# Three moves in a two-stage kernel: one x turned by crossbar, one attention started four steps later, one v loaded later

## The chip, the cores and the metric

The kernel runs on one core of a Trainium2 chip. The core has TensorE (PE, matmuls; its weight loads are shown apart as PEld), VectorE (DVE), ScalarE (ACT), GpSimd (POOL) and SyncE (SP). POOL and SP here mostly issue DMAs, which run on the core's 16 DMA engines. The metric is the device time of one execution in microseconds, lower being better; the figure used is the median of several executions.

## What is computed

Attention over four batches and eight heads, and then two matrix products with a leaky ReLU between them:

```python
# q, k, v: (4, 8, 768, 64); three "retrieval" heads (0, 2, 6) see all earlier keys,
# the other five see the first 4 keys ("sink") and the last 64 ("window")
scores = scale * np.matmul(q, k.transpose(0, 1, 3, 2))
...
scores = np.where(mask[None, :, :, :], scores, -1000000000.0)
scores = scores - np.max(scores, axis=-1, keepdims=True)
a = np.exp(scores)
a = a / (np.sum(a, axis=-1, keepdims=True) + 1e-09)
out = np.matmul(a, v)
...
x = out.transpose(0, 2, 1, 3).reshape(3072, 512)
h = x @ w_in                      # 512 -> 2048
g = np.maximum(0.01 * h, h)
return g @ w_out                  # 2048 -> 512
```

## The kernel before, in words

The 3,072 tokens are cut into eight chunks of 384, two for each batch, in the order of the list ORDER: chunks 0 and 1 are the first halves of batches 0 and 1, chunks 2 and 3 their second halves, then the same for batches 2 and 3. Every chunk goes through attention, product 1 (x times w_in, with the leaky ReLU on ScalarE) and product 2 (times w_out). The schedule is written out by hand: each stage is a list of small functions ("slots"), and helpers merge the lists, so that the order in the program is the order on each engine. Each engine works through its instructions in that order.

**Attention of a chunk** (class Attention, method slots). A unit is one group of scores. For a retrieval head in the second half of a batch there are five groups, in the first half two; a window head has one; and there is one sink group for all heads. That makes 21 units in a second half and 12 in a first half. A unit has two parts. qk makes the scores on TensorE into one bank of the tag psS, which has two banks (lines 329 and 364, sink line 309), has ScalarE take the exponential (lines 334, 369, 312), and has VectorE multiply by a mask where one is needed (lines 337, 339, 373). do_av, a few slots later (the lag), multiplies by v on TensorE (line 298, "sums" below). When the last unit of a pair of heads is through, finish divides by the sum on VectorE (lines 395 and 397) and leaves xs, with tokens on the partitions. Product 1 needs it turned, with features on the partitions; x_t does that, in one of two ways. On TensorE it makes three transposes against the identity into a bank (line 407), and ScalarE (line 409) or VectorE (line 411) copies the bank to xt. That takes place three slots after finish. With cross set, one DMA transpose issued from SP (line 402, the "crossbar") moves xs to xt at once, and the three extra slots are not there. Before the change chunks 1 to 3 turn x on TensorE (chunk 2 with ScalarE's copy, into the banks ph; chunk 3 with VectorE's, into the banks py), and chunks 4 to 7 by crossbar.

**Product 1** (in_slots) has 16 slots of four matmuls of 128x384 (line 563) into one of two banks ph; ScalarE applies the leaky ReLU (line 565). **Product 2** (out_slots) has 16 slots, called steps below, of two to four matmuls of 128x512 (line 589); 16 matmuls make a tile of 128 tokens. When a tile is whole, VectorE copies it to SBUF (line 595) and SP writes it out (line 596).

**Loads.** load_qk and load_v issue loads of k, q and v on POOL's queue (lines 113 and 118). turn_dma turns k and q with two DMA transposes on SP (line 228). spreads gives six copies on VectorE (line 237) that put the turned keys into the two key tiles kt, and for a first half two small ones of the sink keys (lines 262 and 266). v_shift makes, with two DMAs on SP (lines 145 and 146), the copy vb of v shifted by 64 tokens, which window heads read.

**The main loop** runs n from 2 to 7. Round n merges product 1 of chunk n and what is left of product 2 of chunk n - 1 with the attention of chunk n + 1. Its loads run ahead: it issues the turn, the shift and the spreads for chunk n + 2, and the loads of chunk n + 3. Ahead of the loop chunk 2's attention (a2) is merged with steps of product 2 of chunks 0 and 1 (o0 and o1). The merging deals the slots of attention evenly before the steps:

```python
want = (j + 1) * len(as_) // len(ms)
r += as_[done:want] + [m]
```

tail interleaves the last slots of two lists, and both joins a slot with one of the copies of spreads, which is how chunk 4's key copies stand inside chunk 3's attention before the change. into puts such copies between the slots of later attentions.

Of the kernel before, what the change touches and what calls it, by code (L numbers as in the profile page):

```python
# [21 lines left out]
def kernel(  # L22
# [12 lines left out]
    nc = tc.nc  # L35
# [23 lines left out]
    def bank(tag, shape, dtype):  # L59
        return ps.tile(shape, dtype, name=tag, tag=tag, bufs=BANKS[tag])  # L60

    def bf(name, *shape):
        return one.tile([128, *shape], BF16, name=name)
# [14 lines left out]
    m_win = bf("m_win", 6, 64)  # L78
    m_win0 = bf("m_win0", 6, 64)
    m_sink = bf("m_sink", H)  # L80
    shift = bf("shift", 2, 128)
    kt = [[bf(f"kt{i}_{hh}", 4, S) for hh in range(2)] for i in range(2)]
    va = [bf(f"va{i}", 6, H, D + 1) for i in range(B)]
# [23 lines left out]
    def load_qk(n, nms="kq"):  # L107
        b, c = ORDER[n]
        for nm in nms:
            t = rot.tile([128, 3, H, D], BF16, name=f"{nm}b", tag=f"{nm}b", bufs=1)  # L110
            raw[nm, n] = t
            for g in range(3):
                nc.gpsimd.dma_start(out=t[:, g], in_=nat[nm][b, c, :, :, g])  # L113

    def load_v(n, gs=range(3)):
        b, c = ORDER[n]
        for g in gs:
            nc.gpsimd.dma_start(out=va[b][:, 3 * c + g, :, 0:D], in_=nat["v"][b, c, :, :, g])  # L118
# [3 lines left out]
    def load_sinks(b, eng=None):  # L122
        vsf[b] = rot.tile([32, D], FP32, name="vsf", tag="vsf", bufs=2)
        (eng or nc.sync).dma_start(out=vsf[b][:], in_=v[b, :, 0:NS, :])

    def sink_values(b, eng):
        n = H - 1
        eng.tensor_tensor(
            vs[b % 2][0:32, 1:H, 0:D],
            vsf[b].rearrange("p (o d) -> p o d", o=1).to_broadcast([32, n, D]),  # L130
            m_sink[0:32, 1:H].rearrange("p (h o) -> p h o", o=1).to_broadcast([32, n, D]),
            op=ALU.mult)
# [8 lines left out]
    def v_shift(n, eng=None):  # L141
        eng = eng or nc.sync
        i, c = ORDER[n]
        lo, hi = (0, 2) if c == 0 else (2, 5)
        eng.dma_start(out=vb[i][0:64, lo:hi], in_=va[i][64:128, lo:hi])
        eng.dma_start(out=vb[i][64:128, lo:hi], in_=va[i][0:64, lo + 1 : hi + 1])
# [77 lines left out]
    def turn_dma(n):  # L224
        qx[n] = rot.tile([128, 3, 4, 128], BF16, name="qd", tag="qd", bufs=3)
        raw["kx", n] = rot.tile([128, 3, 4, 128], BF16, name="kd", tag="kd", bufs=2)
        for nm, dst in (("k", raw["kx", n]), ("q", qx[n])):
            nc.sync.dma_start_transpose(out=dst.rearrange("p g q t -> p (g q) t"),
                                        in_=raw[nm, n].rearrange("p g h d -> p (g h d)"))

    def spreads(n):
        b, c = ORDER[n]

        def spread(g, hh):
            r = slice(64 * hh, 64 * hh + 64)
            o = CH * c + 128 * g
            nc.vector.tensor_copy(kt[b % 2][hh][r, :, o : o + 128], raw["kx", n][r, g])  # L237

        r = [lambda g=g, hh=hh: spread(g, hh) for g in range(3) for hh in range(2)]
        if c == 0:  # L240
            r += sink_keys_by(b)
        return r
# [4 lines left out]
    def into(slots, extra):  # L247
        r, extra = [], list(extra)
        for j, s in enumerate(slots):
            r.append(s)  # L250
            if 5 * j >= 2 * len(slots) and extra:
                r.append(extra.pop(0))
                if len(extra) > len(slots) - j - 2:
                    r.append(extra.pop(0))
        return r + extra
# [19 lines left out]
    xts = {}  # L275
# [279 lines left out]
    py = {}  # L555

    def in_slots(n, tags=("ph",)):
        def tick(t):
            if n not in gs:
                gs[n] = rot.tile([128, NG, CH], BF16, name="g", tag="g", bufs=2)  # L560
            ph = bank(tags[t % len(tags)], [128, 512], FP32)
            for g in range(KG):
                nc.tensor.matmul(ph[:, 0:CH], lhsT=w_in_bf[:, g, 128 * t : 128 * t + 128],  # L563
                                 rhs=xts[n][:, g, :] if n else xts[0][:, :, g, :], start=(g == 0), stop=(g == KG - 1))
            nc.scalar.activation(out=gs[n][:, t, :], in_=ph[:, 0:CH], func=ACTF.Prelu, alpha=0.01)  # L565

        return [lambda t=t: tick(t) for t in range(NG)]
# [14 lines left out]
    def out_slots(n, tags=("py", "py", "py"), halves=False):  # L582
        slots = []

        def part(tt, lo, hi, tag, c0, c1):
            if lo == 0:
                py[n] = bank(tag, [128, 512], FP32)
            for ng in range(lo, hi):
                nc.tensor.matmul(py[n][:, 0 : c1 - c0], lhsT=gs[n][:, ng, 128 * tt : 128 * tt + 128],  # L589
                                 rhs=w_out_bf[:, ng, c0:c1], start=(ng == 0), stop=(ng == NG - 1))  # L590
            if hi == NG:
                o = rot.tile([128, DM], FP32, name="o", tag="o", bufs=6)
                b, c = ORDER[n]
                r0 = S * b + CH * c + 128 * tt
                nc.vector.tensor_copy(o[:, 0 : c1 - c0], py[n][:, 0 : c1 - c0])  # L595
                nc.sync.dma_start(out=out[r0 : r0 + 128, c0:c1], in_=o[:, 0 : c1 - c0])

        for tt in range(3):
            if halves and tt == 2:
                slots.append(lambda: part(2, 0, NG, "py", 0, 256))  # L600
                slots.append(lambda: part(2, 0, NG, "psS", 256, 384))
                slots.append(lambda: part(2, 0, NG, "po", 384, 512))
                continue
            lo = 0
            for w in ([3, 3, 3, 3, 4], [3, 3, 3, 3, 4], [3, 3, 3, 3, 2, 2])[tt]:
                slots.append(lambda tt=tt, lo=lo, w=w: part(tt, lo, lo + w, tags[tt], 0, DM))
                lo += w
        return slots

    def run(*lists):  # L610
        for l in lists:
            for f in l:
                f()

    def tail(ms, a):

        return [a[0], ms[0], a[1], ms[1], a[2], ms[2], ms[3], *a[3:]]

    def both(s, e):
        return lambda: (s(), e and e())  # L620

    def merge(ms, as_):

        r, done = [], 0
        for j, m in enumerate(ms):
            want = (j + 1) * len(as_) // len(ms)
            r += as_[done:want] + [m]
            done = want
        return r + as_[done:]
# [152 lines left out]
    o0, o1 = out_slots(0), out_slots(1)  # L782
# [1 line left out]
    run(spreads(2))  # L784
    run(o0[6:12])
    v_shift(3)
    a2, m2 = Attention(2, xt_tag="ph").slots(lag=3), o0[12:] + o1[0:10]
    run(merge(m2[:10], a2[:-6]), tail(m2[10:], a2[-6:]))
    run(spreads(3))
    outs = o1[10:]  # L790

    for n in range(2, NCH):
        a, extra = [], ()
        if n + 2 < NCH:
            turn_dma(n + 2)
            v_shift(n + 2)
            extra = spreads(n + 2)
            if ORDER[n + 2][1] == 0:
                load_sinks(ORDER[n + 2][0], nc.gpsimd)
                sink_values(ORDER[n + 2][0], nc.gpsimd)  # L800
            if n + 3 < NCH:
                load_qk(n + 3)
                load_v(n + 3)
        if n + 1 < NCH:
            a = Attention(n + 1, xt_eng="v", xt_tag="py", cross=n > 2).slots(lag=2 if n > 2 else 3)
            a = into(a, extra) if n > 2 else a
        ms = merge(in_slots(n), outs)
        keep = []
        if n == 2:
            a = [both(s, e) for s, e in zip(a, [None] * 16 + extra + [None] * 3)]  # L810
            ms, a, keep = ms[:-6], a[:-6], tail(ms[-6:-2], a[-6:]) + ms[-2:]
        elif a:
            ms, keep = ms[:-9], ms[-9:]
            if n > 4:
                keep.insert(1, a.pop())
        run(merge(ms, a), keep)
        outs = out_slots(n) if n + 1 < NCH else out_slots(n, ("psS", "psS", "py"), True)
    run(outs)

# [34 lines left out]
```

## Time and profile before

| What | us |
|---|---|
| median of 5 runs (lowest 233.71, highest 235.93) | 234.3 |
| the profiled execution, whole | 235.93 |
| its span, from first to last instruction | 234.1 |
| TensorE busy | 226.7 |
| ScalarE busy | 127.7 |
| VectorE busy | 98.0 |
| POOL busy | 71.3 |

The profile shows one execution. Times of single rows are microseconds from the start of the span; a row of a timeline gives start, duration, engine, line, operation and how many equal instructions it merges, and in brackets how long the engine was idle before it and what released it. Matmuls are pipelined: the duration of a row has a fixed latency in it, and the time that a matmul takes from its engine is the distance to the start of the next. These are the stretches that the change touches:

| Stretch, us | What runs on TensorE |
|---|---|
| 48 to 56 | product 2 of chunk 0 alone |
| 56 to 73 | chunk 2's attention with product 2 of chunks 0 and 1 |
| 73 to 95 | round 2: chunk 3's attention, product 1 of chunk 2, rest of product 2 of chunk 1 |
| 95 to 120 | round 3: chunk 4's attention, product 1 of chunk 3, product 2 of chunk 2 |
| 120 to 145 | round 4: chunk 5's attention, product 1 of chunk 4, product 2 of chunk 3 |

### The profile page before, as it was taken

Reading aid. Unit: us, or ns where it says so; the run is one execution under the profiler, and the core shown is the slowest. Engines: PE = TensorE matmul, PEld = TensorE weight load, DVE = VectorE, ACT = ScalarE, POOL = GpSimd, SP = SyncE. Lnnn points to the kernel's source line nnn. Section 1 sums busy time; section 2 is a strip of 40 time slices with the busy share of each in tenths; the row PEclk is TensorE's granted clock in tenths of the full one; section 3 lists DMA queues with packets and bytes.
Section 4 is the critical chain, followed back from the end, with each engine's and each line's share of the span. In section 5 each row is a group of like instructions: output and inputs, shape, how many; then the busy total and the mean of one; then the engine's idle time right before and its main releaser. Section 6 shows DMA issues by size and latency. Waiting matters only on the chain.

```text
span 234.1 us, 5117 instructions
## 1 busy us (share of the span) xinstructions
PE 226.7 (97%) x2080; PEld 140.9 (60%) x2080; DVE 98.0 (42%) x282; ACT 127.7 (55%) x275; POOL 71.3 (30%) x87
## 2 busy tenths in 40 slices
PE   7888999999999999999999999999999999999995
PEld 5668776644665676566556665666656665555554
DVE  7793668115465358446313551156211351111122
ACT  5765875722774786655355545765556763434300
POOL 8967544118419239359004900000000000000000
PEclk9997999999999999999999999999999999999999
DMA  9999999999999999999959991920220221111112
GB/s 129 148 166 178 203 207 168 177 122 154 141 213 230 178 174 122 183 165 164 127 120 184 173 164 44 221 72 17 64 62 0 64 74 25 45 45 45 44 49 91
DMA packets 109480, 28.98 MB, mean 124 GB/s; under 512 B 101248, under 2 KB 105744, under 8 KB 109456
## 3 DMA queue, kind: packets, MB, share of 16 engines
q0 software_dynamic: 77088, 13.39, 75.7%
q1 hardware_dynamic: 31312, 15.00, 31.4%
q10 hardware_dynamic: 1056, 0.26, 0.5%
q8 instruction: 16, 0.26, 0.5%
q14 instruction: 8, 0.07, 0.1%
HBM read 27.30 MB, written 6.29 MB: 143 GB/s over the span
## 4 chain that ended last, share of the span: by engine, by line
PE 88%; POOL 4%; DMA 4%; DVE 2%; ACT 1%; issue 1%; POOLq 0%
PE py L589 32%; PE ph L563 29%; PE po L298 6%; PE psS L329 6%; DMA kb<-in_k_dram 4%; PE psS L589 3%; PE psS L364 3%; PE ph L576 2%; PE psS L563 2%; PE psS L309 2%; POOL va L118 1%; POOL k L104 1%; POOL q L105 1%; DVE xs L397 1%; POOL kb L113 1%; ACT at L334 1%
## 5 line engine op out<-in xcount | busy, mean ns | idle before, releaser
L589 PE MATMUL py<-w_out_bf,g 128*128 128x512 bf16 (+1 forms) x352 | 90.6, 374 | 0.0
L563 PE MATMUL ph<-xt,w_in_bf 128*128 128x384 bf16 x448 | 90.4, 326 | 0.0
L565 ACT ACTIVATE g<-ph 128x384 bf16<-128x384 f32 x112 | 55.0, 491 | 57.2 <-PE ph L563 56.9
L563 PEld LDWEIGHTS <-w_in_bf 128*128 128x128 bf16 x480 | 44.0, 98 | 30.7
L589 PEld LDWEIGHTS <-g 128*128 128x128 bf16 x416 | 35.8, 98 | 25.9
L334 ACT ACTIVATE at<-psS 128x384 bf16<-128x384 f32 x78 | 37.1, 488 | 17.4 <-PE psS L329 16.9
L595 DVE COPY o<-py 128x512 f32<-128x512 f32 (+1 forms) x22 | 14.9, 679 | 52.4 <-PE py L589 52.1
L113 POOL DMA_DIRECT2D kb<-in_k_dram x21 | 18.7, 906 | 37.2 <-DMA kd<-kb 36.5
L329 PE MATMUL psS<-qd,kt 128*128 128x384 bf16 (+2 forms) x90 | 23.3, 294 | 0.0
L118 POOL DMA_DIRECT2D va<-in_v_dram x24 | 21.4, 911 | 4.2 <-DVE xs L544 2.0
L113 POOL DMA_DIRECT2D qb<-in_q_dram x21 | 18.6, 908 | 5.6 <-DMA w_in_bf<-in_moe_w_in_dram 1.8
L298 PE MATMUL po<-va,at 128*128 128x65 bf16 x228 | 19.3, 194 | 0.0
L373 DVE TENSOR_TENSOR ats<-ats,m_win 128x384 bf16<-128x384 bf16 x35 | 13.2, 381 | 13.5 <-ACT ats L369 12.8
L369 ACT ACTIVATE ats<-psS 128x384 bf16<-128x384 f32 x35 | 16.9, 490 | 3.2 <-PE psS L364 2.9
L298 PEld LDWEIGHTS <-at 128*128 128x128 bf16 x234 | 14.9, 98 | 5.2 <-issue 0.2
L397 DVE TENSOR_TENSOR xs<-po,linv 128x384 bf16<-128x384 f32 x27 | 15.1, 557 | 0.9
L329 PEld LDWEIGHTS <-kt 128*128 128x128 bf16 x99 | 9.5, 98 | 7.7 <-issue 0.6
L364 PEld LDWEIGHTS <-kt 128*128 128x128 bf16 x210 | 10.5, 98 | 5.1 <-issue 0.2
L339 DVE TENSOR_TENSOR at<-at,m_caus 128x128 bf16<-128x128 bf16 x21 | 4.8, 240 | 20.6 <-ACT at L334 20.4
L237 DVE COPY kt<-kd 64x512 bf16<-64x512 bf16 x36 | 12.9, 359 | 0.6
L298 PEld LDWEIGHTS <-ats 128*128 128x128 bf16 x210 | 10.4, 97 | 4.1 <-DVE xs L397 0.4
L337 DVE TENSOR_TENSOR at<-at,m_caus 128x256 bf16<-128x256 bf16 x21 | 6.3, 298 | 14.7 <-ACT at L334 14.7
(145 smaller groups left out, 209.8 us busy)
## 6 DMA issues: line engine op xcount, KB each, us to landing
out_dram<-o SPq DMA_DIRECT2D x23, 256.0 KB, 2.4
va<-in_v_dram POOLq DMA_DIRECT2D x24, 128.0 KB, 7.4
kb<-in_k_dram POOLq DMA_DIRECT2D x21, 128.0 KB, 5.8
qb<-in_q_dram POOLq DMA_DIRECT2D x21, 128.0 KB, 5.8
w_in_bf<-in_moe_w_in_dram POOLq DMA_DIRECT2D x4, 512.0 KB, 9.8
w_out_bf<-in_moe_w_out_dram POOLq DMA_DIRECT2D x4, 512.0 KB, 13.6
vb<-va SPq DMA_DIRECT2D x8, 195.0 KB, 4.1
vb<-va SPq DMA_DIRECT2D x4, 130.0 KB, 3.5
```

The costliest lines, as they stand in the source:

```text
L113: nc.gpsimd.dma_start(out=t[:, g], in_=nat[nm][b, c, :, :, g])
L118: nc.gpsimd.dma_start(out=va[b][:, 3 * c + g, :, 0:D], in_=nat["v"][b, c, :, :, g])
L298: nc.tensor.matmul(o, lhsT=lhsT, rhs=rhs, start=first, stop=False, skip_group_check=True)
L329: nc.tensor.matmul(s[:, off : off + w], lhsT=kt[i][hh][:, p, 128 * kj : 128 * kj + 128], rhs=q_of(n, p, lo, CH), start=(j == 0), stop=(j = ...
L334: nc.scalar.activation(out=a[:, 0:off], in_=s[:, 0:off], func=ACTF.Exp, scale=SM)
L364: nc.tensor.matmul(s[:, 64 * m : 64 * m + 64], lhsT=kt[i][hh][:, p, k0 : k0 + 128], rhs=q_of(n, p, 64 * m, 64 * m + 64), start=(m == 0), s ...
L369: nc.scalar.activation(out=av_, in_=s[:, 0:CH].rearrange("p (j e f) -> p j e f", j=3, e=2), func=ACTF.Exp, scale=SM)
L397: nc.vector.tensor_tensor(xs[:], po[:, :, :, 0:D], linv.to_broadcast([128, 3, 2, D]), op=ALU.mult)
L563: nc.tensor.matmul(ph[:, 0:CH], lhsT=w_in_bf[:, g, 128 * t : 128 * t + 128], rhs=xts[n][:, g, :] if n else xts[0][:, :, g, :], start=(g == ...
L565: nc.scalar.activation(out=gs[n][:, t, :], in_=ph[:, 0:CH], func=ACTF.Prelu, alpha=0.01)
L589: nc.tensor.matmul(py[n][:, 0 : c1 - c0], lhsT=gs[n][:, ng, 128 * tt : 128 * tt + 128], rhs=w_out_bf[:, ng, c0:c1], start=(ng == 0), stop= ...
L595: nc.vector.tensor_copy(o[:, 0 : c1 - c0], py[n][:, 0 : c1 - c0])
```

## The change

Chunk 3's attention is built with cross set: its x is turned by four crossbar DMAs on SP instead of twelve transposes on TensorE and four copies on VectorE. Its list of slots has 24 entries instead of 27. Chunk 2's x is still turned on TensorE, but VectorE makes the copy instead of ScalarE. Ahead of the loop chunk 2's attention is merged with two steps fewer of chunk 1's product 2; they go to round 2. There the eight copies of chunk 4's keys no longer stand among the slots of chunk 3's attention but after all of the round's slots. Round 3 begins with four steps of chunk 2's product 2 alone, then merges four more, and product 1 of chunk 3 comes after these eight. Chunk 6's v is not loaded together with its q and k at the start of round 3; at the end of the round POOL copies one element of chunk 4's last part of xt to a new tile named hold, which makes the queue wait for that part to land, and then issues the load.

```diff
+    hold = bf("hold", 1)
...
-    def both(s, e):
-        return lambda: (s(), e and e())
...
-    a2, m2 = Attention(2, xt_tag="ph").slots(lag=3), o0[12:] + o1[0:10]
-    run(merge(m2[:10], a2[:-6]), tail(m2[10:], a2[-6:]))
+    a2, m2 = Attention(2, xt_tag="ph", xt_eng="v").slots(lag=3), o0[12:] + o1[0:8]
+    run(merge(m2[:8], a2[:-6]), tail(m2[8:], a2[-6:]))
     run(spreads(3))
-    outs = o1[10:]
+    outs = o1[8:]
...
                 load_qk(n + 3)
-                load_v(n + 3)
+                if n != 3:
+                    load_v(n + 3)
         if n + 1 < NCH:
-            a = Attention(n + 1, xt_eng="v", xt_tag="py", cross=n > 2).slots(lag=2 if n > 2 else 3)
+            a = Attention(n + 1, cross=True).slots(lag=2 if n > 2 else 3)
             a = into(a, extra) if n > 2 else a
-        ms = merge(in_slots(n), outs)
+        if n == 3:
+            run(outs[:4])
+            ms = outs[4:8] + merge(in_slots(n), outs[8:])
+        else:
+            ms = merge(in_slots(n), outs)
         keep = []
         if n == 2:
-            a = [both(s, e) for s, e in zip(a, [None] * 16 + extra + [None] * 3)]
-            ms, a, keep = ms[:-6], a[:-6], tail(ms[-6:-2], a[-6:]) + ms[-2:]
+            ms, a, keep = ms[:-6], a[:-3], tail(ms[-6:-2], a[-3:]) + ms[-2:]
...
-        run(merge(ms, a), keep)
+        run(merge(ms, a), keep, extra if n == 2 else ())
+        if n == 3:
+
+            nc.gpsimd.tensor_copy(hold[0:1, :], xts[n + 1][0:1, 3, 0:1])
+            load_v(n + 3)
```

## The prediction, written before the changed kernel was run

> **What bounds the kernel now.** I read the page's busy table first, then the granted clock, then TensorE's timeline from 48 us on for places where it stands still, and last the views of the engines that release it there.
>
> ```profile
> PE 226.7 (97%) x2080; PEld 140.9 (60%) x2080; DVE 98.0 (42%) x282; ACT 127.7 (55%) x275; POOL 71.3 (30%) x87
> ...
> PEclk9997999999999999999999999999999999999999
> ```
>
> TensorE (PE) is busy 97% of the span, at full clock but for one slice near 20 us, and the diff changes no instruction before 56 us. From there the end is TensorE's own work plus the moments when it stands still. Its row durations overlap, so I count from start to start: a 128x512 matmul takes 0.216 us (352 of them), 128x384 takes 0.162, 128x128 0.056, a sum of 65 columns 0.029. By these steps TensorE stands still for only 1.26 us between 48 us and the end: 0.15 (57.77), 0.06 (65.13), 0.23 (68.83), 0.09 (74.09), 0.06 and 0.13 (76.18 and 76.42), 0.47 (94.07) and 0.07 at 166. Two of these places matter. The first is in chunk 2's attention:
>
> ```profile
> 67.93 0.33 PE L329 MATMUL psS<-qd,kt 128*128 128x384 bf16 x1
> 68.09 0.25 PE L298 MATMUL po<-va,at 128*128 128x65 bf16 x3
> 68.18 0.33 PE L407 MATMUL ph<-ident,xs 128*128 128x128 bf16 x3
> 68.35 0.33 PE L329 MATMUL psS<-qd,kt 128*128 128x256 bf16 x2
> 68.51 0.26 PE L298 MATMUL po<-va,at 128*128 128x65 bf16 x3
> 68.83 0.34 PE L364 MATMUL psS<-qd,kt 128*128 128x64 bf16 x6
> ```
>
> ```profile
> 68.29 0.49 ACT L334 ACTIVATE at<-psS 128x384 bf16<-128x384 f32 x1 [0.85 <-PE psS L329]
> ```
>
> Scores rotate over two banks (psS). The score at 67.93 is read by ScalarE from 68.29 to 68.78, and the next but one, into the same bank, starts at 68.83 though TensorE had finished its steps by 68.51 + 3 x 0.029 = 68.60. So a score can follow the one two before it only 0.90 us later (0.36 to ScalarE, 0.49 there, 0.05 back). The second place is the end of chunk 3's attention:
>
> ```profile
> 92.30 1.46 PE L563 MATMUL ph<-xt,w_in_bf 128*128 128x384 bf16 x8
> 94.07 0.34 PE L407 MATMUL py<-ident,xs 128*128 128x128 bf16 x3 [0.31 <-DVE xs L397]
> 94.25 0.59 PE L589 MATMUL py<-w_out_bf,g 128*128 128x512 bf16 x2
> ```
>
> Eight matmuls from 92.30 are through at 93.60; the transposes start at 94.07, when VectorE has made xs.
>
> **Chunk 3's x by crossbar.** Twelve transposes (line 407) leave TensorE. Three take 0.17 us (88.60 to 88.77, 89.94 to 90.11): 12 x 0.056 = -0.67. The wait at 94.07 goes with them: -0.47. Four copies of 0.35 (line 411) leave VectorE, which bounds nothing. SP gains four transposes. They stand behind chunk 4's turn, its shift of v and an output, free from about 87; the first three pairs go there. The last pair's xs comes at about 93.4: sums finished at 92.4, reciprocal and product 0.20 + 0.56, nothing ahead of them on VectorE. After those sums TensorE has 9.2 us to do before chunk 3's product 1: three tiles of it for chunk 2 (1.95), 27 product-2 matmuls (5.83) and chunk 4's first scores and sums (1.45); the pair is read by the fourth matmul, 0.49 later. So it may take 8.6 us from issue. The view of line 402 has the price:
>
> ```profile
> L402 SPq DMA_TRANSPOSE xt<-xs x16: 1177/1180/2233, 102.9 to 196.2; - x16
> ...
> DMA to landing us min/median/max: 2.3/3.8/7.0
> ```
>
> All sixteen would be in time, so I take 0. The upper bound is the longest landing of the larger transposes (line 228), 11.1 us: 2.5 us late. Behind the pair on SP stand an output and chunk 5's turn; that output was issued at 95.60 before, and chunk 1's last tile is copied out at about 95.0 now, so these do not move later.
>
> The Trainium skill, page "VectorE: DVE Perf Modes", section "Rules for kernel authors", speaks against this part: transpose 128x128 on TensorE if a PSUM destination will do. The same page's section "The three transpose paths" has 390 ns there and 1309 ns by crossbar. The row says 56 ns of TensorE's time in a full queue. By the page's figure the part would be worth 12 x 0.39 = 4.7 us, an estimate; by the row 0.67.
>
> **Two product-2 steps out of chunk 2's attention.** m2 falls from 14 steps to 12, the merged ones from ten to eight, for the same 21 slots of attention. Before, a step (0.43 to 0.86 us of matmuls) stood after every two slots, and only the last group had three. Now five groups have three scores without a step between, and each third one meets the bank rule. The matmuls between first and third score are: slots 2 to 4, 0.56 with the second score's own wait of 0.15; slots 7 to 9, two scores and nine sums 0.59; slots 10 to 12, 0.50; slots 15 to 17, 0.76; slots 18 to 20, 0.67. The rest to 0.90 is lost: 0.34 + 0.31 + 0.40 + 0.14 + 0.23 = 1.42, and with the 0.15 that stays, 1.57. Before these were 0.15 + 0.06 + 0.23 = 0.44. This part costs +1.13. The bounds are 0 (the waits hide) and 1.13 plus 1.4, should the four copies of chunk 2's x, now VectorE's at 0.35 instead of ScalarE's at 0.49, stand ahead of masks that the sums wait for. VectorE is busy 7.0 of the 16 us from 56 to 72, and a mask is ready some 0.5 us before its sum, so I take 0 for the copies. The 0.06 at 65.13 came from such a copy on ScalarE and is in the sum.
>
> The removed steps run later: 0.65 us each wherever they stand, 0 in sum. In chunk 3's attention 18 tiles stand among 21 slots instead of 16, so no three scores meet. At its start 0.28 goes: x's last copy is 0.14 shorter, more than the 0.09 waited at 74.09, and chunk 3's six key copies (2.70 us from 73.99) no longer stand behind an output's copy of 0.69, which ends the 0.06 and 0.13.
>
> **Chunk 4's keys and its four steps.** The eight copies (six of 0.27 to 0.72, two of 0.54 and 0.16) move behind chunk 3's xs and an output's copy, to about 95.0. The first score that reads them comes after twelve matmuls (2.6 us), at about 97.4; it needs the first copy, done by 95.7. The third score group and the sink score have more. Cost 0. Without the four steps the score would come at 94.8 and wait 0.9. Those steps are the same matmuls, moved.
>
> **Chunk 6's v.** On POOL one element is copied when x(4) has landed (about 118), and three loads of 0.9 us follow, instead of at 108.55. Behind them on POOL are chunk 7's k and q, which waited for kd until 126.36 anyway. v lands after 4.3 to 14.2 us (line 118), so by 125 to 135. Behind it on SP stands the shift of v (125.11 before), then x(5), whose first pair went at 127.66 and whose last at 139.92. Chunk 5's product 1 starts at 145.93 and chunk 6's vb is read at 151.11. Even 135 leaves ten us. Cost 0. No gain either: x(4) landed 118.93 and was read from 120.95.
>
> **Sum.** -0.67 - 0.47 - 0.28 + 1.13 = -0.29 us. The span goes from 234.1 to 233.8. The profiled execution took 235.93 (1.83 around the span), so 235.6; it was the longest of the five runs. Against their median of 234.3 I subtract the same: 234.0.
>
> **Rivals.** First, the thinned attention costs nothing: -1.42, or 232.9. For it: ScalarE is busy only 10.25 of 16 us there, so on average it keeps up. Against it: 68.83 shows the wait in the one group of three that exists. Second, and on the other side, chunk 3's x lands late. The place is the fourth matmul of its product 1. The cost begins 8.6 us after issue, and it decides from 10.1 us on. At 11.1 us the time is 234.0 + 2.5 = 236.5. For it: loads of chunk 5's k, q and v and its turn share the DMA engines, busy over 90% in these slices, and larger transposes needed 11.1. Against it: sixteen of the same size had 7.0 at most, some under the same load. Third, the copies on VectorE delay sums: up to 1.4, or 235.4. Against it are the idle stretches of VectorE there. Fourth, the late load of v does nothing, as I count it; were it to speed up x(4), nothing waits for that.
>
> **How the numbers follow.** A measurement of this kernel tells 0.5% from no change, 1.17 us: below 233.1 is faster, above 235.5 slower. My forecast has 0.60 (own range 233.5 to 234.6), the first rival 0.22, the second 0.13, the third 0.05. Faster is the first rival, 0.22. Slower is the second and the third, 0.18: the third's full price ends within 0.1 us of the line, and I count it there. The rest is no change. The predicted time is 234.0. The range reaches down past the first rival, 232.7, and up to 235.3, near the third; the second stays out.
>
> **What would show it.** Right: no line 407 after 80 us and no wait near 94; five waits of 0.1 to 0.4 us between scores of line 329 and 364 from 57 to 69; product 1 of chunk 3 starting without a gap at about 101.6; v of chunk 6 landing after 122 with no gap after it. Wrong: scores in groups of three running without waits (then 232.9), or a gap before line 564 near 101 released by a DMA (then 235 and more).

## The result and the profile after

| | before | after |
|---|---|---|
| median, us | 234.03 (90 runs) | 234.58 (48 runs) |
| ratio, 95% interval | | 1.0036 [1.0023, 1.005] |
| the profiled execution, us | 235.93 | 234.35 |
| its span | 234.1 | 232.6 |
| first score of chunk 2's attention, from the start of the span | 56.48 | 55.02 |
| from there to the start of the last matmul ("middle") | 174.60 | 174.25 |
| from there to the end of the span ("tail") | 3.06 | 3.31 |

The change makes the kernel slower by 0.84 us (0.36% of 234.03; 0.54 to 1.17 by the interval). That is less than the 0.5% which the prediction called no change, but it is resolved, and its sign is not that of the forecast: 0.29 us less. The profiled execution of before happened to be a long one, with a granted clock of 0.97 instead of 1.00 before 56 us, so spans of single executions say little here. The medians are over all runs and lie only 0.55 us apart, while the ratio leaves disturbed executions out and counts that after has more long ones (17 of 48 above 235.3 us, against 8 of 90). The middle, which holds all that the diff moves, is 0.35 us shorter after, close to the 0.29 that was predicted from the same row of before; but these are two single executions, and over four traces of each the difference is 0.06 (see "What is left").

The first lines are of the page of after.

```profile
span 232.6 us, 5101 instructions
...
PE 224.5 (97%) x2068; PEld 138.9 (60%) x2068; DVE 96.4 (41%) x282; ACT 127.1 (55%) x271; POOL 71.8 (31%) x88
...
PEclk9999999999999999999999999999999999999999
```

TensorE has 12 instructions fewer, the transposes. It is still busy 97%, so the same way of counting holds: start to start, and what exceeds the steps of the prediction is standing still. The kernel after has one line more ahead of everything, so line 329 is now 330, and so on.

TensorE's timeline of after in chunk 2's attention (start, duration, engine, line, operation, and in brackets the idle time and its releaser):

```profile
61.07 0.33 PE L330 MATMUL psS<-qd,kt 128*128 128x256 bf16 x2
61.24 0.25 PE L299 MATMUL po<-va,at 128*128 128x65 bf16 x3
61.72 0.34 PE L365 MATMUL psS<-qd,kt 128*128 128x64 bf16 x6 [0.23 <-ACT at L335]
...
66.47 0.33 PE L330 MATMUL psS<-qd,kt 128*128 128x256 bf16 x2
66.63 0.26 PE L299 MATMUL po<-va,at 128*128 128x65 bf16 x3
66.95 0.34 PE L365 MATMUL psS<-qd,kt 128*128 128x64 bf16 x6
```

Three sums from 61.24 are through at 61.24 + 3 x 0.029 = 61.33; the score starts at 61.72, 0.40 later, released by the exponential. The pair at 66.63 and 66.95 loses 0.23 in the same way. All the waits of this stretch are 0.15 (56.30), 0.34 (56.89), 0.30 (59.84 and 60.14), 0.40, 0.13 (64.89) and 0.23: 1.55, where the prediction has 1.57 at the same five places and the one that stays.

Where product 1 of chunk 3 begins, in TensorE's timeline of after:

```profile
100.35 0.20 PE L299 MATMUL po<-va,ats 128*128 128x65 bf16 x1
100.39 0.81 PE L564 MATMUL ph<-xt,w_in_bf 128*128 128x384 bf16 x4
101.03 0.33 PE L330 MATMUL psS<-qd,kt 128*128 128x256 bf16 x2
```

The first matmul follows its neighbour by 0.04 and the four of them take 0.64: no wait for the x that the crossbar turns. SP's view has the four DMAs, and behind them the output and chunk 5's turn:

```profile
85.73 7.61 SPq L403 DMA_TRANSPOSE xt<-xs  x4
93.79 0.34 SPq L597 DMA_DIRECT2D out_dram<-o  x1
94.30 3.47 SPq L229 DMA_TRANSPOSE kd<-kb  x1
```

They landed at 92.3, 93.9, 96.2 and 99.1, the last 6.9 us after its issue at 92.2, where the prediction allowed 8.6.

One place that the prediction passed over is tight now. TensorE and POOL of after, where chunk 4's product 1 begins:

```profile
118.98 0.33 PE L330 MATMUL psS<-qd,kt 128*128 128x384 bf16 x1
119.14 0.81 PE L564 MATMUL ph<-xt,w_in_bf 128*128 128x384 bf16 x4
119.79 0.33 PE L330 MATMUL psS<-qd,kt 128*128 128x256 bf16 x2
```

```profile
119.25 0.18 POOL L821 COPY hold<-xt 1x1 bf16<-1x1 bf16 x1 [9.28 <-DMA xt<-xs]
119.49 2.64 POOL L119 DMA_DIRECT2D va<-in_v_dram  x3
```

POOL's copy of one element stands behind the landing of chunk 4's last part of x, and runs at 119.25. The fourth matmul of 119.14, which reads that part, starts 0.49 later, at 119.63. About 0.4 us are left. Before, x had landed at 118.93, 2.0 us ahead of the first of these matmuls.

### The profile page after: what moved, and what is told of

Its sections match the earlier page's. It is cut to its first block, busy times and chain, and to the rows that moved or that the text cites. A ratio compares the mean times of both kernels' runs of the same rounds, so it can differ in the third digit from the quotient of the medians.

```text
span 232.6 us, 5101 instructions
## 1 busy us (share of the span) xinstructions
PE 224.5 (97%) x2068; PEld 138.9 (60%) x2068; DVE 96.4 (41%) x282; ACT 127.1 (55%) x271; POOL 71.8 (31%) x88
## 4 chain that ended last, share of the span: by engine, by line
PE 89%; POOL 4%; DMA 3%; DVE 1%; ACT 1%; issue 0%; POOLq 0%
PE py L590 32%; PE ph L564 31%; PE po L299 7%; PE psS L330 5%; DMA kb<-in_k_dram 3%; PE psS L590 3%; PE psS L365 3%; PE psS L564 2%; PE ph L577 2%; PE psS L310 2%; POOL va L119 1%; ACT at L335 1%; POOL k L105 1%; POOL q L106 1%; POOL kb L114 1%; DVE xs L398 0%
## 5 line engine op out<-in xcount | busy, mean ns | idle before, releaser
L564 PE MATMUL ph<-xt,w_in_bf 128*128 128x384 bf16 x448 | 89.5, 326 | 0.0
L374 DVE TENSOR_TENSOR ats<-ats,m_win 128x384 bf16<-128x384 bf16 x35 | 12.4, 358 | 12.5 <-ACT ats L370 12.1
L396 DVE RECIPROCAL linv<-po 128x6 f32<-128x6 f32 x27 | 5.2, 193 | 17.4 <-PE po L299 17.3
```

## The experiments

Eighteen runs were made in five groups, each group beside its own runs of the kernel before; five of them (after_again, before_again and the three labels in _b) repeat a kernel. At first the question was which part makes the kernel slower than the sum: the thinned attention, the crossbar, x of chunk 4 or 5 arriving late in executions that the profile does not show (theory 2 of the expectations), or none of the scheduled parts. Later the new tile came under suspicion: it stands early among the tiles and moves those behind it by 32 bytes.

### The parts, one at a time

**steps_only**: the kernel before, with only the steps taken out.

```diff
-    a2, m2 = Attention(2, xt_tag="ph").slots(lag=3), o0[12:] + o1[0:10]
-    run(merge(m2[:10], a2[:-6]), tail(m2[10:], a2[-6:]))
+    a2, m2 = Attention(2, xt_tag="ph").slots(lag=3), o0[12:] + o1[0:8]
+    run(merge(m2[:8], a2[:-6]), tail(m2[8:], a2[-6:]))
...
-    outs = o1[10:]
+    outs = o1[8:]
```

> The kernel before with one edit: chunk 2's attention is merged with eight product-2 steps instead of ten (the two others run in round 2). Theory 1 (scores in groups of three wait for their bank): the waits between scores from 56 to 69 us go from 0.44 to about 1.5 us and the time from 234.0 to 235.0. Theory 2 (the changed kernel loses its time on late DMAs in rounds 3 and 4, the waits between scores are made up for elsewhere): no change, 234.0.

Measured: 235.0 beside 233.88, ratio 1.0042 [1.002, 1.0065], +1.0 us (0.5 to 1.5). The trace has the five waits of after to 0.01 us. One of them in TensorE's timeline of steps_only:

```profile
60.22 0.33 PE L329 MATMUL psS<-qd,kt 128*128 128x256 bf16 x2
60.38 0.25 PE L298 MATMUL po<-va,at 128*128 128x65 bf16 x3
60.87 0.34 PE L364 MATMUL psS<-qd,kt 128*128 128x64 bf16 x6 [0.23 <-ACT at L334]
```

The three sums are through at 60.47 and the score starts 0.40 later, released by the exponential, as in after. The mechanism and its price, 1.13, hold.

**steps_back**: the kernel after, with 14 steps there again.

```diff
-    a2, m2 = Attention(2, xt_tag="ph", xt_eng="v").slots(lag=3), o0[12:] + o1[0:8]
-    run(merge(m2[:8], a2[:-6]), tail(m2[8:], a2[-6:]))
+    a2, m2 = Attention(2, xt_tag="ph", xt_eng="v").slots(lag=3), o0[12:] + o1[0:10]
+    run(merge(m2[:10], a2[:-6]), tail(m2[10:], a2[-6:]))
...
-    outs = o1[8:]
+    outs = o1[10:]
```

> The changed kernel with the two product-2 steps back in chunk 2's attention. Theory 1: the waits of 1.55 us fall to about 0.45, the time from 234.6 to 233.5, which is below the kernel before. Theory 2 (chunk 4's x lands within half a microsecond of its first use, and later than that in many executions): TensorE only comes sooner to a x that is as late as before, less than half of the gain is seen, 234.2 to 234.6.

Measured: 234.13 beside 233.88, ratio 1.001 [0.9984, 1.0037]. That is 0.6 us below after, give or take 0.7; the 233.5 of theory 1 was not reached. The waits of chunk 2's attention are 0.15 and 0.23 again, 1.17 less than in after, but the middle is 173.53, only 0.72 below that of after: a new wait of 0.39 has come, and one of 0.06. TensorE's and VectorE's timelines of steps_back:

```profile
71.47 0.65 PE L564 MATMUL ph<-xt,w_in_bf 128*128 128x384 bf16 x3
72.35 0.32 PE L564 MATMUL ph<-xt,w_in_bf 128*128 128x384 bf16 x1 [0.23 <-DVE xt L412]
```

```profile
71.34 0.69 DVE L596 COPY o<-py 128x512 f32<-128x512 f32 x1 [0.72 <-PE py L590]
71.95 0.35 DVE L412 COPY xt<-ph 128x384 bf16<-128x384 bf16 x1
```

Three matmuls from 71.47 end at 71.96; the fourth reads the last part of chunk 2's x and waits until 72.35 for VectorE's copy of it, which stood behind an output's copy. In after there is no such wait.

**no_cross**: the kernel after, with chunk 3's x on TensorE.

```diff
-            a = Attention(n + 1, cross=True).slots(lag=2 if n > 2 else 3)
+            a = Attention(n + 1, xt_eng="v", xt_tag="py", cross=n > 2).slots(lag=2 if n > 2 else 3)
...
-            ms, a, keep = ms[:-6], a[:-3], tail(ms[-6:-2], a[-3:]) + ms[-2:]
+            ms, a, keep = ms[:-6], a[:-6], tail(ms[-6:-2], a[-6:]) + ms[-2:]
```

> The changed kernel with chunk 3's x turned on TensorE again (twelve transposes, four copies on VectorE). Theory 1: the transposes come back, 0.67 us, and no wait for xs, since the key copies stay behind: 235.2. Theory 4 (the four crossbar transposes slow chunk 5's loads and with them all that follows on POOL and SP): less than the 0.67 is seen, or a gain, 234.0 to 234.6.

Measured: 235.16 beside 233.88, ratio 1.0054 [1.0023, 1.0084], against 1.0036 for after. The middle is 174.97, 0.72 more than after's: 12 transposes at 0.06, and no wait of over 0.06 near 94. The median agrees with that but its interval holds zero too.

**v6_early**: the kernel after, with chunk 6's v loaded at the start of the round.

```diff
-                if n != 3:
-                    load_v(n + 3)
+                load_v(n + 3)
...
-            nc.gpsimd.tensor_copy(hold[0:1, :], xts[n + 1][0:1, 3, 0:1])
-            load_v(n + 3)
```

> The changed kernel with chunk 6's v loaded where it was before, and without the hold copy. Theory 2: chunk 4's x is turned among more loads and lands later still, 235.0 or more, with a wait near 119 us at line 558 or so (product 1 of chunk 4). Theory 3 (the late load pushes chunk 7's loads onto chunk 5's x): faster by 0.3 to 0.8, 233.8 to 234.3. Theory 1 alone: no change, 234.6.

Measured: 237.11 beside 233.88, ratio 1.0118 [1.0077, 1.0159]. TensorE's timeline of v6_early:

```profile
119.27 0.65 PE L564 MATMUL ph<-xt,w_in_bf 128*128 128x384 bf16 x3
122.21 0.32 PE L564 MATMUL ph<-xt,w_in_bf 128*128 128x384 bf16 x1 [2.29 <-DMA xt<-xs]
```

Three matmuls are through at 119.76, and the fourth starts 2.45 us later, when the last part of chunk 4's x has come. Its transpose was issued at 113.4, as in after (113.3), and what waited for it started 8.8 us later instead of 6.0. Beside after's ratio the time is 1.9 us longer (0.0082 x 234.03), give or take 1.0, about the size of the wait, for a load that the prediction gave nothing.

### Is it the place of tiles in memory?

**pad32**: the kernel before with one line, the tile that nothing uses. **pad64**: the kernel after with the tile 64 bytes large. **back_pad64** and **v6_early_pad64**: steps_back and v6_early with the larger tile.

```diff
+    hold = bf("hold", 1)
```

That is pad32; the other three have:

```diff
-    hold = bf("hold", 1)
+    hold = bf("hold", 32)
...
-            nc.gpsimd.tensor_copy(hold[0:1, :], xts[n + 1][0:1, 3, 0:1])
+            nc.gpsimd.tensor_copy(hold[0:1, 0:1], xts[n + 1][0:1, 3, 0:1])
```

> The kernel before, with only the tile hold added, which nothing uses. Its 2 bytes take 32 in every partition, and all tiles allocated after it (keys, v, weights, x, outputs) start 32 bytes later: on odd multiples of 32 bytes, where they stood on multiples of 64. Theory 5 (the shift makes the DMAs into and out of these tiles slower): the same instructions take 234.5 to 235, loads and crossbar land later, and the share of time of the software queue's packets rises from 75.7% towards 84.5%. Without theory 5: no change, 234.0.

> The changed kernel with hold made 64 bytes long, so that all tiles after it stand on multiples of 64 bytes again, as in the kernel before; the work is the same. Theory 5: the time falls from 234.6 to about 233.7, what the sum of the prediction gives without the shift, and the tail above 235 gets thin. Without theory 5: no change, 234.6.

> The changed kernel with both mended: the two product-2 steps back in chunk 2's attention, and hold 64 bytes long. Theories 1 and 5 together: about 1.1 below the last one, 232.6, faster than the kernel before by 0.6%. Theory 1 alone: as the run with the steps back, 234.1.

> The changed kernel with chunk 6's v loaded early again and no hold copy, but the tile hold kept, 64 bytes long. Theory 5: chunk 4's x lands sooner than in the run with the 32-byte shift, where TensorE waited 2.3 us for it; 237.1 falls to 234 to 235.5. Without theory 5: 237.1 again, the whole wait comes from the early load.

Measured, beside 234.02: pad32 235.01, ratio 1.0021 [0.9996, 1.0046]; pad64 235.03, 1.0038 [1.0011, 1.0064]; back_pad64 234.03, 0.9997 [0.9968, 1.0027]; v6_early_pad64 237.83, 1.0137 [1.0083, 1.0191]. Moving by 64 bytes in place of 32 changes nothing (pad64 is at 1.0038, after at 1.0036), so a particular alignment (theory 5) falls. But the tile alone, which adds no instruction, may cost 0.2%. The wait for chunk 4's x stands in v6_early_pad64, too, where v is again loaded early: 1.34 us from start to start in this execution.

### Is it chunk 4's or 5's x?

**after_again** is the kernel after unaltered. **slack4** gives round 4, too, four steps of product 2 ahead of the rest; **back_slack45** is steps_back with that in rounds 4 and 5.

```diff
-        if n == 3:
+        if n in (3, 4):
             run(outs[:4])
```

> The changed kernel unaltered, as the reference for the two others and for a second profile. Theory 2 (crossbar transposes land late in a part of the executions): median 234.6, about a third of its times above 235; if its profile is of such an execution, a wait for a DMA stands before product 1 of chunk 4 or 5 (near 119 or 144 us).

> The changed kernel with round 4 begun like round 3: four product-2 steps alone and four more merged ahead of product 1 of chunk 4, so that chunk 4's x has some 7 us more to land. The same matmuls in another order. Theory 2: the waits for chunk 4's x go, the median falls by 0.3 to 0.6 below that of the changed kernel beside it, with few times above 235.5. If late x is not the cause: no change.

> The changed kernel with the two product-2 steps back in chunk 2's attention and rounds 4 and 5 begun like round 3, so that neither chunk 4's nor chunk 5's x can be late. Theories 1 and 2 together: 1.1 less from the scores and 0.3 to 0.6 less from late x, 233.0 to 233.3, faster than the kernel before. If only theory 1 holds: 233.5 to 234.1, as the run with the steps back.

Measured, beside 233.98: after_again 234.45, ratio 1.0043 [1.0011, 1.0074]; slack4 235.58, 1.0071 [1.0028, 1.0114]; back_slack45 234.03, 0.9997 [0.997, 1.0023]. The result repeats. Round 4 holds product 1 of chunk 4, so slack4 gives chunk 4's x more room (in its trace x lands at 119.7 and product 1 starts at 127.3), and back_slack45 that of chunks 4 and 5. slack4 is not faster than after, where theory 2 had put it 0.3 to 0.6 us below, so for chunk 4's x theory 2 falls. For chunk 5's x the answer is weaker. In the eleven traces with the crossbar, v late and round 5 as in after, it lands 2.9 to 7.1 us after its issue, in ten of them 0.04 to 3.6 us ahead of the matmul that reads it, and once too late. TensorE's timeline of back_pad64:

```profile
144.28 0.65 PE L564 MATMUL ph<-xt,w_in_bf 128*128 128x384 bf16 x3
145.41 0.32 PE L564 MATMUL ph<-xt,w_in_bf 128*128 128x384 bf16 x1 [0.48 <-DMA xt<-xs]
```

From start to start that is 0.64 lost. In v6_early and v6_early_pad64, with v early, chunk 5's x is 4.2 us ahead, and in back_slack45 4.2 too. But back_slack45 stands only 0.1 us below the three runs of steps_back and back_pad64, give or take 0.8: a cost of some tenths from chunk 5's x, in part of the executions, is neither shown nor excluded.

### The tile, taken out

**after_diff**: the kernel after without the tile; the one element goes into a tile that exists, so every address is that of before. **back_diff**: the same with the 14 steps. **pad32_b** and **before_again**: pad32 and the kernel before once more.

```diff
-    hold = bf("hold", 1)
...
-            nc.gpsimd.tensor_copy(hold[0:1, :], xts[n + 1][0:1, 3, 0:1])
+            nc.gpsimd.tensor_copy(diff[0:1, 0:1], xts[n + 1][0:1, 3, 0:1])
```

> The changed kernel without the tile hold: POOL's one-element copy goes into diff, a setup tile that nobody reads any more, so every tile stands at the address it has in the kernel before. Theory 6 (any shift of the tiles lengthens the first 55 us, where TensorE waits for the first loads): first score of chunk 2 at about 54.5 us instead of 55 to 55.8, median 0.5 to 0.8 below the changed kernel, 233.9 to 234.1. Otherwise: 234.5, as the changed kernel.

> As the last one, with the two product-2 steps back in chunk 2's attention. Theory 6 with theory 1: 233.2 to 233.4, faster than the kernel before by 0.3%. Theory 1 without theory 6: 234.1, as the earlier run with the steps back.

> The kernel before with the unused tile hold once more, since its interval reached from no change to 0.5%. Theory 6: again 234.5 to 235, with its lowest times above the lowest of the kernel before. Otherwise: 234.0.

> The kernel before against itself: ratio 1, and how far twelve runs can stray from it by chance; a second profile of it for the wait of 0.47 us at 94 us (0.12 in the run with the unused tile) and for the first score of chunk 2.

Measured, beside 233.68: after_diff 234.16, ratio 1.0024 [1.0001, 1.0047]; back_diff 233.44, 0.9981 [0.9955, 1.0006]; pad32_b 234.12, 1.0025 [1.0001, 1.0049]; before_again 233.67, 0.9992 [0.9961, 1.0024]. Again the kernels with the tile are above their twins, by less than the intervals. Theory 6 looked for the loss ahead of 55 us: the first scores come at 54.98 (after_diff), 53.85 (back_diff), 55.42 (pad32_b) and 54.46 (before_again). The order fits, but the spread among all traces is larger (back_diff_b of the next group, without the tile, has 55.94), so this is not shown.

### The last three

**best2** is back_diff with ScalarE making chunk 2's copies, as before; **back_diff_b** and **steps_back_b** are repeats, side by side.

```diff
-    a2, m2 = Attention(2, xt_tag="ph", xt_eng="v").slots(lag=3), o0[12:] + o1[0:10]
+    a2, m2 = Attention(2, xt_tag="ph").slots(lag=3), o0[12:] + o1[0:10]
```

> The change without its steps taken from chunk 2's attention (14 steps there, as before), without the new tile (the one element goes into a tile that exists), and with chunk 2's x copied by ScalarE as before. In the kernel of this kind whose copies VectorE made, TensorE waits 0.39 us at about 72 for the last of those copies. If that wait is the copy's engine, it is gone and the time is 0.2 to 0.4 us below that kernel's (back_diff_b), some 233.1 beside 233.8 of the kernel before, ratio 0.997. If it is the place of the copy's slot, the wait stays and the two are equal.

> The kernel of back_diff once more: the change without its steps taken from chunk 2's attention and without the new tile. If it is faster than the kernel before, its ratio is again near 0.998; if the first measurement was chance, it is near 1.000.

> The kernel of steps_back once more, beside back_diff_b on the same chip; the two differ only in the new tile and the 32 bytes by which it moves what comes after it in memory. If the tile alone costs, this one is 0.2 to 0.3% above back_diff_b (ratio near 1.001); if the tile costs nothing, the two are equal.

Measured, beside 233.64: best2 233.66, ratio 1.0003 [0.997, 1.0037]; back_diff_b 233.77, 0.9981 [0.995, 1.0012]; steps_back_b 233.46, 1.0001 [0.9969, 1.0033]. TensorE's timeline of best2 at the wait that steps_back had:

```profile
72.33 0.90 PE L563 MATMUL ph<-xt,w_in_bf 128*128 128x384 bf16 x4
73.07 0.32 PE L329 MATMUL psS<-qd,kt 128*128 128x384 bf16 x1
```

The four matmuls take 0.74 instead of 0.65: the wait is 0.09, not 0.39, so 0.30 of it was VectorE's. The middle is the shortest of all, 173.33, but the time is not below back_diff's; the expected 0.2 to 0.4 us is not shown. Neither is any version shown to be faster than the kernel before: the two runs of back_diff are at 0.9981 and both intervals reach past 1.

Three pairs of programs differ only in the tile. With the runs of a program weighted by their intervals, the tile adds 0.0031 to the kernel before (pad32, pad32_b against before_again), 0.0013 to after (after, after_again, pad64 against after_diff) and 0.0022 to steps_back (three against the two of back_diff). Together that is 0.0020, give or take 0.0016: about 0.5 us, 0.1 to 0.9. No pair shows it alone; the nearest are pad32 and pad32_b, which by their own ratios stand 0.0023 above the kernel before, give or take 0.0017. And the traces do not show where it would be: pad32 and pad32_b have middles of 174.10 and 174.26, not longer than 174.60 and 174.56 in the two traces of before.

## Why the prediction was right, and where it failed

**The bank rule, right.** 1.57 of waits predicted, 1.55 in the trace; 1.13 of cost predicted, 1.55 - 0.44 = 1.11 in the trace and +1.0 us in steps_only (0.5 to 1.5). The first rival, that the thinned attention costs nothing, falls with it.

**Twelve transposes, right.** -0.67 predicted; 0.72 by the middle of no_cross, one trace (the ratios differ by 0.4 us, give or take 0.8). The Trainium skill, page "VectorE: DVE Perf Modes", section "The three transpose paths", by whose figure of 390 ns the part would be worth an estimated 4.7 us, does not fit a full queue of TensorE: the measurement decides. Chunk 3's x was not late in any of the fourteen traces with the crossbar, so the second rival, 236.5, did not come.

**The wait at 94, failed as a term of the sum.** "The wait at 94.07 goes with them: -0.47." It goes, but 0.47 was one execution's. The traces of before_again and of pad32_b, whose instructions are those of before, have at the same place:

```profile
90.34 1.46 PE L563 MATMUL ph<-xt,w_in_bf 128*128 128x384 bf16 x8
92.01 0.34 PE L407 MATMUL py<-ident,xs 128*128 128x128 bf16 x3 [0.21 <-DVE xs L397]
```

```profile
91.83 0.98 PE L564 MATMUL ph<-xt,w_in_bf 128*128 128x384 bf16 x5
92.67 0.34 PE L408 MATMUL py<-ident,xs 128*128 128x128 bf16 x3
```

Eight matmuls from 90.34 are through at 91.64, so 0.37 is lost in the first; five from 91.83 are through at 92.64, so 0.03 in the second. In pad32 it is 0.12. The mean of the four is 0.25, half of what was put down. Nor need it be the crossbar that takes the wait away. no_cross keeps the transposes and has the key copies behind the round, and its one trace has no wait there either (eight matmuls from 91.39 are through at 92.69):

```profile
91.39 1.46 PE L564 MATMUL ph<-xt,w_in_bf 128*128 128x384 bf16 x8
92.69 0.33 PE L408 MATMUL py<-ident,xs 128*128 128x128 bf16 x3
```

**The start of chunk 3's attention, right.** -0.28 predicted. The same three waits are 0.34, 0.40 and 0.15 in before_again, pad32_b and pad32, a mean of 0.29 with the 0.28; after has none there.

**Chunk 6's v, wrong in its reason.** "Cost 0. No gain either", and in the fourth rival "nothing waits for that". v is in time, as predicted (landed 125.6 to 129.1), though chunk 5's x, which is turned after it, becomes tight (back_pad64 above). But the prediction took chunk 4's x from the trace of before, where it came 3.8 us after issue, and did not ask what the other parts do to it. POOL's copy, which waits for this x, shows what becomes of it in after and in no_cross:

```profile
119.25 0.18 POOL L821 COPY hold<-xt 1x1 bf16<-1x1 bf16 x1 [9.28 <-DMA xt<-xs]
```

```profile
116.05 0.18 POOL L821 COPY hold<-xt 1x1 bf16<-1x1 bf16 x1 [8.53 <-DMA xt<-xs]
```

The transpose was issued at 113.3 and 113.7, so x took 6.0 us with chunk 3's x on the crossbar and 2.3 without. The other traces, up to the landing or the start of what waited for it, give 3.0 to 5.1 us in the five with chunk 3's x on TensorE and v early (before, before_again, pad32, pad32_b, steps_only); 2.6 to 6.5, with a mean of 4.9, in the twelve with the crossbar and v late; and 8.8 and 7.7 in the two with the crossbar and v early. So the wait comes where the crossbar and the early v meet, and the load's new place is what lets the rest of the change run without it. The DMA columns of the tables by stage do not tell the kernels apart. The stretch from 95 to 120 us of before, after and pad32 (the stretch; busy time and count of PE, PEld, DVE, ACT and POOL; clock; packet time of all DMA queues in shares of the 16 engines; GB/s):

```profile
95.00:120.00 25.00, 25.00 (x215) 14.84 (x213) 10.39 (x31) 12.81 (x28) 9.45 (x11) 1.00 1.60 154
```

```profile
95.00:120.00 25.00, 25.00 (x216) 15.02 (x215) 11.34 (x35) 13.70 (x30) 7.00 (x9) 1.00 1.97 154
```

```profile
95.00:120.00 25.00, 25.00 (x215) 14.83 (x213) 11.30 (x31) 12.91 (x29) 8.92 (x10) 1.00 1.90 155
```

Before and after differ, 1.60 and 1.97, but pad32, with the instructions of before, has 1.90; the means of the five and the twelve traces are 1.60 and 1.61.

**The tail, left out.** The prediction ended its sum at the last matmul. The last copy on VectorE and the end of the span, before and then after:

```profile
core 0 of [0], span 234.1 us
...
231.34 0.29 DVE L595 COPY o<-po 128x128 f32<-128x128 f32 x1 [0.60 <-PE po L589]
```

```profile
core 0 of [0], span 232.6 us
...
229.52 0.29 DVE L596 COPY o<-po 128x128 f32<-128x128 f32 x1 [0.60 <-PE po L590]
```

From the end of that copy to the end, the last output on its way, are 234.1 - 231.63 = 2.5 and 232.6 - 229.81 = 2.8. The six traces with chunk 3's x on TensorE have tails of 3.06 to 3.28 (mean 3.14), the fourteen others 3.31 to 3.62. Why an output at 230 us should care what was turned at 92 was not examined.

**What is left.** With measured terms the middle is -0.72 - 0.25 - 0.29 + 1.11 = -0.15, instead of -0.29. Read whole, it differs by less still: 174.60, 174.56, 174.10 and 174.26 in before, before_again, pad32 and pad32_b, and 174.25, 174.36, 174.25 and 174.42 in after, after_again, after_diff and pad64, a difference of -0.06 between the means. The tails of the same traces add 0.2. So the step that failed is the sum: of its terms, -0.47 for the wait at 94 measures 0.25, and the tail, put at nothing, costs 0.2. With these two put right the gain is gone, and about +0.1 is left where -0.29 stood.

The measured +0.84 (0.54 to 1.17) is 0.7 more than that, and its cause stays open. The unused tile may hold 0.5 (0.1 to 0.9) of it, but that is an estimate from pooled runs, not a cause shown, and after_diff, which does without the tile, is still at 1.0024, +0.56. The time outside the span is 1.7 to 1.95 us in every profiled execution, so the rest would lie ahead of chunk 2's first score, or in waits that only some executions have, such as the 0.64 for chunk 5's x in back_pad64. The first score comes at 55.25 on average in the thirteen traces with the tile and at 55.03 in the seven without, in a spread of 3.3, which shows nothing.

As the chances were put, no change within 0.5%, 0.60, was the right case, and 234.58 lies in the range, at the upper end of the forecast's own; the sign below that line was wrong. Some of the nearness is luck: 234.0 was counted from 234.3, the median of five runs, and from the 234.03 of ninety the same sum gives 233.74.

**The third rival** (VectorE's copies hold up sums) did not come. Of the 0.30 near 60, 0.19 was sums at 59.84 waiting for the shifted v, a DMA issued at 54.5 that landed 5.2 us later (after_again names it as the releaser), and 0.11 the score at 60.14; in no_cross and pad64 the same 0.31 stands ahead of that score alone, released by the exponential, so the bank would have cost it anyway. In back_pad64 that v landed at 60.35 and the sums stood still for 0.87. VectorE's copies do cost 0.30 at 72, but only with the steps back.

## What to carry to other kernels

Where an engine is busy 97%, count its waits start to start and take each wait that a change removes from several executions: 0.47 in one was 0.25 on average, and the 0.22 between them is most of the 0.29 that was forecast. Taking work away from between scores that share two banks costs whatever is then missing to the turn of a bank, here 0.90 us from a score to the next but one, and that can be read off the trace to a few hundredths. When a change adds DMAs, measure again the landing of every transfer that is read soon after, also of those that the change does not touch.

## What was not expected of the hardware

The first 55 us vary more than the change is worth, though no instruction differs there: the first score of chunk 2 came between 53.9 and 57.2 us in the twenty traces of this study. The page of slack4 has one of the long ones, and its TensorE timeline the wait ahead of it:

```profile
PEclk9997999999999999999999999999999999999999
```

```profile
17.76 0.23 PE L204 MATMUL psS<-ident,kb 128*128 128x128 bf16 x1 [1.13 <-DMA kb<-in_k_dram]
18.64 0.23 PE L204 MATMUL psS<-ident,kb 128*128 128x128 bf16 x1 [0.66 <-DMA kb<-in_k_dram]
19.19 0.40 PE L204 MATMUL psS<-ident,kb 128*128 128x128 bf16 x4 [0.32 <-DMA kb<-in_k_dram]
```

TensorE stands still for 2.1 us in three pieces while k loads, and the granted clock of the slice from 17.6 to 23.5 us is 0.7; the trace of before has the same slice at 0.7, the other pages none. Both have late first scores, 57.17 and 56.48.

The second thing is the tile: a line that allocates 32 bytes and does nothing else appears to cost about 0.2%, with an interval that stays clearly above zero only when runs are pooled, and with no place in the trace.
